# An FFT filter and a SiLU MLP in one kernel: a third staging buffer for the output weights, x behind the input weights, and part of the first MLP stretch moved one step later

## The chip, the cores and the metric

The kernel runs on one core of a Trainium2 chip. The metric is the device time of one execution in microseconds (us). The kernel before takes 776.0 us (median of 4 runs, 775.89 to 776.11). The profile counts a span from the first to the last instruction, which is 1.7 to 2.0 us shorter than the time. Ratios are computed as the mean time of one kernel's runs over that of the other's runs, so they are not quite the ratios of the medians that I quote.

PE is the matmul engine and PEld its weight load; DVE is VectorE, ACT is ScalarE, POOL is GpSimd, and SP is the engine that issues most DMAs.

## The reference

```python
X = np.fft.rfft(x, axis=1)                    # x: 8 x 3008 x 256
y = np.fft.irfft(X * (filt_r + 1j * filt_i)[None], n=3008, axis=1)
t = y.reshape(8 * 3008, 256)
h = t @ w_in                                  # 256 -> 2048
g = h * (1.0 / (1.0 + np.exp(-beta * h)))
out = g @ w_out                               # 2048 -> 256
```

## The kernel before

A prologue of about 33 us builds the transform tables and filters the first of eight batches. The MLP then runs as 752 steps; a step is one block of 128 hidden features for 512 tokens. In each step PE computes `hps` (two matmuls), ACT applies SiLU, and two steps later PE adds four `acc` matmuls with `w_out`. The transforms of the next batch are woven between them by a table of steps (`at(step, function, ...)`).

What the change touches: the output weights are loaded in four blocks of 512 KB into staging buffers (`ws`), and POOL divides each by beta into `wout_sb`; the input weights and x come by POOL's own DMA queue; the last units of the first batch's transform are finished inside the MLP ("late" turns: `z_late` is eight transposes on PE, called the z transposes here, and `f_late` the matmuls that read their result); `s1` is the first transform stage of the second batch and reads x (`xg`).

```python
wst = ctx.enter_context(tc.tile_pool(name="wstage", bufs=2, **tw))
...
for u in range(4):
    spread(u)                       # POOL copies of filter rows, each waits for filter loads
load_win(0, 4 * P)                  # input weights of steps 0 to 3, 256 KB
spread(4)
spread(5)
load_x(1, 0)
load_win(4 * P, FF)                 # input weights of steps 4 to 15, 768 KB
for g in range(1, 4):
    load_x(1, g)
load_wout(0)                        # SP's queue
load_wout(WG)
scale_wout(0)                       # POOL
scale_wout(WG)
...
at(0, z_late, 1, 0)
at(1, z_late, 1, 1)
s1_steps(1, range(16), [3 + (2 * i + 1) // 3 for i in range(16)], False, (1, 4, 7, 10, 13))
for i, r in enumerate((2, 3, 4, 5)):
    at(r, f_late, 1, i // 2, i % 2)
...
for f in (2, 3):
    at(f, load_wout, f * WG)
    at(f, scale_wout, f * WG)
```

`spin(n)` runs n matmuls on a tile that nobody reads; they fill PE's time just ahead of the MLP.

## Time and profile before

| | before |
|---|---|
| time, median | 776.0 us |
| span of the profiled run | 774.4 us |
| PE busy | 763.8 us (99%) |
| start of the first z transposes | 34.32 us |
| PE's empty issue time just before them | 0.44 us |
| PE's empty issue time at step 10, waiting for output weights | 0.89 us |

How to read it: PE is full nearly everywhere, so only PE's holes can be won. A hole is measured in issue time: the start of the next matmul, less the start of the last one and its usual distance to a successor (0.217 us for 512 columns, 0.109 for 256, 0.043 for 94 or 96). The profile's own "idle before" is shorter, because it counts from the modelled end of a matmul. The prediction shows the lines.

### The profile page before, as it was taken

The page shows a single profiled execution, that of the slowest core. Times are in us where ns is not written, and L with a number is a line of the kernel's source. Part 1 is how long each engine was busy: PE and PEld are TensorE (multiplying, and loading weights), DVE is VectorE, ACT ScalarE, POOL GpSimd, SP SyncE. Part 2 cuts the span into 40 slices and gives each one's busy share as a digit, 9 for nine tenths or more (in the row PEclk, how much of TensorE's full clock was granted, in tenths as well). Part 3 has the DMA queues.
Part 4 walks back from the last instruction along what each step waited for, and adds up shares of the span by engine and source line. Part 5 has one row for each costly group of instructions (what it writes and reads, how often), then busy time and mean ns, then how long its engine had stood idle before and what let it go on. Part 6 is the DMA issues. An engine that isn't in the chain of part 4 may idle for free.

```text
span 774.4 us, 15904 instructions
## 1 busy us (share of the span) xinstructions
PE 763.8 (99%) x6384; PEld 550.2 (71%) x6384; DVE 433.0 (56%) x716; ACT 552.2 (71%) x813; POOL 151.0 (20%) x154
## 2 busy tenths in 40 slices
PE   8899999999999999999999999999999999999997
PEld 5677777767777777867778777776777766676665
DVE  8868754766556655566556664566645665321001
ACT  7767877776677776777667777676676777777776
POOL 6714400312012210122201322022200222000000
PEclk9999999999999999999999999999999999999999
DMA  9968575234923248141671317621147111500101
GB/s 200 210 142 133 145 172 110 69 101 93 200 52 74 91 111 180 39 115 50 144 157 55 91 48 176 123 76 48 49 130 137 49 49 48 157 29 28 55 28 55
DMA packets 104125, 77.74 MB, mean 100 GB/s; under 512 B 49692, under 2 KB 97052, under 8 KB 104052
## 3 DMA queue, kind: packets, MB, share of 16 engines
q1 hardware_dynamic: 97652, 63.19, 31.3%
q0 software_dynamic: 4192, 13.40, 10.3%
q8 instruction: 50, 0.82, 0.4%
q10 hardware_dynamic: 2208, 0.14, 0.2%
q14 instruction: 23, 0.19, 0.1%
HBM read 43.46 MB, written 35.65 MB: 102 GB/s over the span
## 4 chain that ended last, share of the span: by engine, by line
PE 94%; DMA 2%; ACT 1%; DVE 1%; POOL 1%; issue 0%; DVEq 0%; POOLq 0%
PE acc L803 42%; PE hps L785 41%; PE ps L646 2%; PE ps L592 2%; PE ps L624 2%; PE ps L565 2%; DMA ws<-in_moe_w_out_dram 2%; POOL wout_sb L367 0%; PE sps L444 0%; ACT aT L110 0%; ACT t L110 0%; ACT y L110 0%; DVE u L226 0%; POOL xg L171 0%; PE sps L423 0%
## 5 line engine op out<-in xcount | busy, mean ns | idle before, releaser
L794 ACT ACTIVATE gT<-hps,beta_sb 128x512 bf16<-128x512 f32 x752 | 516.6, 687 | 209.4 <-PE hps L785 208.2
L803 PE MATMUL acc<-wout_sb,gT 128*128 128x256 bf16 x3008 | 453.2, 272 | 0.7 <-POOL wout_sb L367 0.7
L785 PE MATMUL hps<-y,win_sb 128*128 128x512 bf16 (+7 forms) x1728 | 447.8, 351 | 0.1
L803 PEld LDWEIGHTS <-gT 128*128 128x128 bf16 x3008 | 281.1, 98 | 102.9 <-issue 1.8
L611 POOL TENSOR_TENSOR yh<-a_t,b_t 128x512 bf16<-128x512 f32 x84 | 106.5, 1268 | 419.9 <-DVE b_t L610 419.5
L785 PEld LDWEIGHTS <-win_sb 128*128 128x128 bf16 x1728 | 164.8, 98 | 24.3 <-DVE y L114 0.3
L112 DVE COPY ost<-acc 128x512 f32<-128x512 f32 (+1 forms) x94 | 59.9, 679 | 139.8 <-PE acc L803 139.8
L114 DVE TENSOR_SCALAR y<-ps 128x376 bf16<-128x376 f32 (+2 forms) x128 | 63.3, 510 | 62.8 <-PE ps L646 59.1
L606 DVE TENSOR_TENSOR a_t<-ps,fr_sb 128x512 f32<-128x512 f32 x84 | 58.1, 692 | 67.8 <-PE ps L592 67.2
L112 DVE CAST a<-ps 128x384 bf16<-128x384 f32 x107 | 59.1, 556 | 58.0 <-PE ps L565 47.5
L607 DVE SCALAR_TENSOR_TENSOR b_t<-ps,fi_sb 64x512 f32<-64x512 f32 x84 | 58.2, 693 | 1.1
L610 DVE TENSOR_TENSOR b_t<-ps,fi_sb 64x512 f32<-64x512 f32 x84 | 57.4, 683 | 1.1
L112 DVE CAST z<-ps 128x512 bf16<-128x512 f32 x72 | 49.3, 685 | 1.9 <-PE ps L624 1.0
L646 PEld LDWEIGHTS <-zz 96*128 96x128 bf16 x448 | 29.7, 97 | 22.9
L565 PEld LDWEIGHTS <-xg 94*128 94x128 bf16 x448 | 30.4, 97 | 19.9
L565 PE MATMUL ps<-t,xg 94*128 94x96 bf16 x448 | 36.7, 205 | 0.0
L646 PE MATMUL ps<-t,zz 96*128 96x94 bf16 x448 | 34.7, 205 | 0.0
L592 PE MATMUL ps<-a,t 128*128 128x256 bf16 x168 | 32.1, 273 | 0.0
L624 PE MATMUL ps<-yh,t 128*128 128x256 bf16 x168 | 32.1, 273 | 0.0
L624 PEld LDWEIGHTS <-t 128*128 128x128 bf16 x168 | 16.2, 98 | 17.7 <-issue 0.6
L592 PEld LDWEIGHTS <-t 128*128 128x128 bf16 x168 | 16.1, 98 | 16.1
L171 POOL DMA_DIRECT2D xg<-in_x_dram x24 | 12.5, 524 | 54.9 <-PE ps L565 54.9
(95 smaller groups left out, 177.3 us busy)
## 6 DMA issues: line engine op xcount, KB each, us to landing
out_dram<-ost SPq DMA_DIRECT2D x42, 512.0 KB, 3.0
d<-z SPq DMA_DIRECT2D x28, 384.0 KB, 3.7
zz<-d SPq DMA_DIRECT2D x28, 384.0 KB, 6.8
xg<-in_x_dram POOLq DMA_DIRECT2D x24, 384.0 KB, 4.8
out_dram<-ost SPq DMA_DIRECT2D x9, 256.0 KB, 3.6
ws<-in_moe_w_out_dram SPq DMA_DIRECT2D x4, 512.0 KB, 9.2
fr_sb<-in_filt_r_dram SPq DMA_DIRECT2D x12, 128.0 KB, 4.4
fi_sb<-in_filt_i_dram SPq DMA_DIRECT2D x12, 128.0 KB, 4.3
```

Of the source, the lines that this page charges most:

```text
L112: nc.vector.tensor_copy(dst, src)
L114: nc.vector.tensor_scalar_mul(dst, src, scale)
L565: nc.tensor.matmul(ps[:, m * KP : (m + 1) * KP], lhsT=xg[b, g][:NP, m0 + m, e * P : (e + 1) * P], rhs=t1[:], start=True, stop=True,)
L592: nc.tensor.matmul(ps[:, e, :], lhsT=t2[:, k0 + e, :], rhs=st["a2", b, g][:, kk + e, :], start=True, stop=True,)
L606: nc.vector.tensor_tensor(a_t[:], ps[:], fr_sb[:, ks, :], ALU.mult)
L607: nc.vector.scalar_tensor_tensor(b_t[:M], ps[M:], -1.0, fi_sb[M:, ks, :], ALU.mult, ALU.mult)
L611: nc.gpsimd.tensor_tensor(yh[:], a_t[:], b_t[:], ALU.add)
L624: nc.tensor.matmul(ps[:, e, :], lhsT=t3[:, 2 * i + e, :P], rhs=yh[:, e, :], start=True, stop=True)
L646: nc.tensor.matmul(ps[:, e, :NP], lhsT=zz[:, j0 % JG + e, dc * P : (dc + 1) * P], rhs=t4[:], start=True, stop=True,)
L785: nc.tensor.matmul(hps[:, pos - t0 : pos - t0 + ln], lhsT=win_sb[:, dc, fb * P : (fb + 1) * P], rhs=ys[b][:, dc, n0 : n0 + ln], start=(dc ...
L794: nc.scalar.activation(gT[:], hps[:], ACT.Silu, scale=beta_sb[:, fb : fb + 1])
L803: nc.tensor.matmul(acc_of(i, tb)[:, tb % 2, :], lhsT=blk[i * NFB + fb][:, tb * P : (tb + 1) * P], rhs=wout_sb[:, fb, :], start=(fb == 0 an ...
```

## The change

The intent is to have the third block of output weights on the chip before PE needs it, to give PE a second pair of `hps` matmuls while VectorE still clears the banks of the prologue, and to make room for x, which now comes after the input weights.

```diff
-    wst = ctx.enter_context(tc.tile_pool(name="wstage", bufs=2, **tw))
+    wst = ctx.enter_context(tc.tile_pool(name="wstage", bufs=3, **tw))
...
-    load_x(1, 0)
     load_win(4 * P, FF)
-    for g in range(1, 4):
+    for g in range(4):
         load_x(1, g)
-    load_wout(0)
-    load_wout(WG)
+    for f0 in range(0, 3 * WG, WG):
+        load_wout(f0)
     scale_wout(0)
     scale_wout(WG)
...
-    spin(2, tail_tile(0, [P, 512]))
+    spin(1, tail_tile(0, [P, 512]))
...
-            at(0, z_late, 1, 0)
-            at(1, z_late, 1, 1)
-            s1_steps(1, range(16), [3 + (2 * i + 1) // 3 for i in range(16)], False, (1, 4, 7, 10, 13))
-            for i, r in enumerate((2, 3, 4, 5)):
+            at(1, z_late, 1, 0)
+            at(2, z_late, 1, 1)
+            s1_steps(1, range(16), [4 + (2 * i + 1) // 3 for i in range(16)], False, (1, 4, 7, 10, 13))
+            for i, r in enumerate((3, 4, 5, 6)):
...
-            for f in (2, 3):
-                at(f, load_wout, f * WG)
-                at(f, scale_wout, f * WG)
+            at(0, scale_wout, 2 * WG)
+            at(0, load_wout, 3 * WG)
+            at(1, scale_wout, 3 * WG)
```

I call the staging buffers part 1, the late turns and the spin part 2, and the new place of x with the later `s1` part 3.

## The prediction

> **What bounds the kernel now.** I read the page first: busy shares, then the chain that ended last.
>
> ```profile
> PE 763.8 (99%) x6384; PEld 550.2 (71%) x6384; DVE 433.0 (56%) x716; ACT 552.2 (71%) x813; POOL 151.0 (20%) x154
> ...
> PE 94%; DMA 2%; ACT 1%; DVE 1%; POOL 1%; issue 0%; DVEq 0%; POOLq 0%
> ```
>
> PE is busy for 99% of the 774.4 us span and is 94% of the chain. The only DMA on the chain is 2%, which the line shares give to the output weights (ws). No step of the MLP is added or removed, so the time can move only where PE stands still. I therefore looked for PE's holes next: the timeline of PE alone, around the start of the MLP (start us, us, engine, line, what, count, idle before).
>
> ```profile
> 32.80 0.60 PE L271 MATMUL pt<-rest 128*128 128x512 bf16 x2
> 33.45 0.59 PE L785 MATMUL hps<-y,win_sb 128*128 128x512 bf16 x2
> 34.32 0.61 PE L393 MATMUL tp<-ident,y 128*128 128x128 bf16 x8 [0.28 <-DVE y L114]
> 34.77 0.59 PE L785 MATMUL hps<-y,win_sb 128*128 128x512 bf16 x2
> 35.20 0.61 PE L393 MATMUL tp<-ident,y 128*128 128x128 bf16 x8
> 35.65 0.59 PE L785 MATMUL hps<-y,win_sb 128*128 128x512 bf16 x2
> 36.08 0.33 PE L398 MATMUL ps<-t,zz 96*128 96x94 bf16 x4
> 36.24 0.60 PE L803 MATMUL acc<-wout_sb,gT 128*128 128x256 bf16 x4
> ...
> 46.32 0.51 PE L565 MATMUL ps<-t,xg 94*128 94x96 bf16 x8
> 47.55 0.60 PE L803 MATMUL acc<-wout_sb,gT 128*128 128x256 bf16 x4 [0.73 <-POOL wout_sb L367]
> ```
>
> Two holes stand here. Differences of starts give what a packed group costs in PE's issue: an hps pair 0.43 (34.77 to 35.20), eight transposes 0.45 (34.32 to 34.77), four acc 0.44 (36.24 to 36.68), four of s1 or of a late turn 0.17 (36.08 to 36.24). The printed idle times count from the modelled end of the matmul before, so they are short. In issue slots the first hole is 34.32 - (33.45 + 0.43) = 0.44 us: the first z transposes wait for VectorE's last evictions from the banks that they reuse. The second is 47.55 - (46.32 + 2 x 0.17) = 0.89 us. From 48 us to the end I found no PE wait over 0.15 us; the waits view lists PE's acc waiting for wout_sb once and nothing else on PE in the MLP. The chain between 31 and 48 us tells what made the second hole:
>
> ```profile
> 31.18 1.90 POOL wout_sb L367
> 33.09 0.02 issue
> 33.10 12.44 DMA ws<-in_moe_w_out_dram
> 45.54 0.07 issue
> 45.61 1.90 POOL wout_sb L367
> 47.51 0.04 issue
> 47.55 0.60 PE acc L803 x4
> ```
>
> The third block of output weights is issued at 33.10, because only two staging buffers exist and the first is free when GpSimd has scaled it. It then takes 12.44 us, where the first took 5.2, and GpSimd needs 1.90 more.
>
> **What the Trainium skill says.** "DMA: Bandwidth & Descriptors", section "Queues, rings and completion order": each DMA engine serves the queue rows that have work in turn, and descriptors of one ring in ring order. The trace agrees in the main: the third block (SP's queue) waits while x and the input weights (GpSimd's queue) drain; its packets run in number only from 37 us and fast only from 43, when the other queue is empty. So a transfer's place in the order decides when it lands. "TensorE: Matmul & The Clock Gate", section "Back-to-back issue gap": about 216 ns between 512-column matmuls at full clock; half of my 0.43 per pair, so these stretches are packed and cannot be compressed. "SBUF — State Buffer", section "SBUF: two separate sides": VectorE and GpSimd lock each other out only where VectorE uses two SBUF ports. The moved scaling meets VectorE copies out of PSUM; the trace shows such a cast of 128x384 at 0.55 us with GpSimd busy (33.34) and 0.56 without (37.49), so I count no cost.
>
> **Part 1: three staging buffers, third load at once.** It is issued after the second, at about 23.5 instead of 33.1, and lies ahead of x. On SP's queue alone 512 KB take about 1.5 us (the queue moved some 0.17 to 0.18 MB per 0.5 us at 44 to 45 us). GpSimd scales three blocks back to back from 31.18: 31.18 + 3 x 1.89 = 36.9. PE needs the third at step 10, about 45. The 0.89 us hole goes. The fourth block is issued at 33.1, when the first buffer is free, so it inherits the old third's slow path: landed by 45.5, scaled by 47.5, needed at step 14, about 51. No new wait; gain 0.89.
>
> **Part 2: late turns a step later, one spin less.** The z transposes cannot start before 34.32, since VectorE's order ahead of them is unchanged. But the hps pair of step 1 now comes before them. With one spin, the first hps is freed about 0.22 earlier (at 33.24; it waits for the end of the last spin in the same bank); its second half waits for y until 33.48; step 1 then fills 33.70 to 34.13, and z starts at 34.32 as before. So 0.43 of useful work is moved into the hole: gain 0.43. The removed spin alone is worth nothing more, since VectorE sets 34.32; with two spins, 33.45 + 0.43 + 0.43 = 34.31 would fit too.
>
> **Part 3: x and the input weights swap places, s1 a step later.** From the landing times of narrow windows of the DMA view (KB each, median us to landing), the input weights issued at 28.8 and the first x at 28.3:
>
> ```profile
> win_sb<-in_moe_w_in_dram POOLq DMA_DIRECT2D x1, 768.0 KB, 8.5
> xg<-in_x_dram POOLq DMA_DIRECT2D x1, 384.0 KB, 4.6
> ```
>
> So before, x0 landed at 32.9 and the weights at 37.3, just in time for hps of step 4 at 37.89. Swapped, the weights land near 35 and x0 last of the pair, near 37.3. PE's order after the change, from 34.32: z 0.45, hps2 0.43, z 0.45, acc0 0.44, hps3 0.43, late turn 0.17, acc1 0.44, hps4 0.43, then s1 at 37.55, its weights loaded from 37.33. So x0 comes at its deadline. Two things move it: the inserted 512 KB push it back by up to 1.5 us, and the hole in the DMA traffic takes them up:
>
> ```profile
> 22.00:27.00 5.00, 4.77 (x61) 3.79 (x60) 5.00 (x5) 4.59 (x6) 4.78 (x6) 1.00 1.00 274
> 28.50:30.50 2.00, 1.77 (x29) 1.44 (x26) 1.56 (x3) 1.02 (x2) 2.00 (x4) 1.00 0.72 76
> ```
>
> The last column is GB/s: in 28.5 to 30.5 only 76 were moved against 274 just before, an idle worth of 2 x (1 - 76/274) = 1.44 us, about what ws needs. I estimate x0 at 37.3 to 37.8 and a new wait of 0.15 us (0 to 0.6). Later x keep their landings (about 39.7, 42.8, 45.2 by the same view) while their users come at steps 7, 9 and 12, about 41.8, 44 and 48, so they are free. The DMA transposes that follow s1 shift by less than a step and land about 5 us ahead of their reader at 61.86. The busier step 6 (s1, late turn and z turn in one) may cost 0.05 by waiting for a PSUM bank.
>
> Sum: -0.89 - 0.43 + 0.15 + 0.05 = -1.12, and PE has no later slack that could swallow it: 776.09 - 1.1 = 775.0.
>
> **Rivals.** (a) x0 is starved: if SP's queue with three weight blocks holds the software queue back (the first input weights, issued at 23.12, took 7.0 us for only 256 KB while SP's queue drained), x0 could land at 38 to 38.5 and PE waits 0.5 to 1.0 at step 4; time 775.4 to 775.9. For it: the deadline is that close. Against: the traffic hole, and the author's shift of s1. (b) The weight wait is only replaced: the fourth block comes too late. It would have to take over 15 us from 33.1; 11.9 and 12.4 were seen. If it did, 775.5 to 776. (c) The gain is lost later to a fixed-time transfer; against it, PE shows no such wait in the rest; would give 776. (d) x0 is early and VectorE frees the banks sooner: full gain, 774.7.
>
> **Range and chances.** The sum of holes caps the gain at 0.89 + 0.44 + 0.22 = 1.55, giving 774.5; (a) and (b) reach 775.9. Runs of one kernel spread by 0.2. Range 774.6 to 775.9. 2% is 15.5 us, ten times all holes together: same 0.98, and 0.01 for each side.
>
> **What would show it.** In the new profile: acc no longer waits for wout_sb, four scalings with the first three back to back ending near 36.9; ws third landing near 30; two hps pairs in a row before the first z transposes at 34.3; the first s1 near 37.6 with at most a short wait for x; the hps of step 4 without a wait for its weights. A wait of over 0.6 us at s1, or a new wait at the scaling of the fourth block, would make it wrong, as would a z start that leaves 34.3.

## The result, and the profile after

The changed kernel took 775.97 us in the median of 4 runs, against 776.0 us before. The ratio is 1.0 with a 95% interval of 0.9983 to 1.0017: the same, as the forecast of the class had it, but the median is 0.07 us outside the predicted range and the expected 1.0 us is missing. The single runs are 775.0, 777.1, 775.71 and 776.22; the four of before lie within 0.22 of each other. The profiled run is the first one, 775.0, which is the predicted time to the digit. So the trace in hand and the median tell different stories, and that is what had to be explained.

First the profiled run. Its page (busy time and instructions by engine; chain by engine):

```profile
PE 757.8 (98%) x6286; PEld 549.6 (71%) x6383; DVE 433.3 (56%) x716; ACT 552.3 (71%) x813; POOL 151.1 (20%) x154
...
PE 96%; ACT 1%; DVE 1%; issue 1%; POOL 0%; DVEq 0%; POOLq 0%
```

The DMA is off the chain. PE's busy time fell by 6 us only because 97 of the 6383 matmul records are missing from this trace (PEld has 6383, PE 6286; the third trace of this kernel has all 6383, and 763.9 us); a hole of exactly one missing matmul is no hole. Line numbers are one lower than before (L802 is the old L803). The timeline of PE in the same stretch, in the same columns as in the prediction:

```profile
32.81 0.38 PE L271 MATMUL pt<-rest 128*128 128x512 bf16 x1
33.24 1.07 PE L784 MATMUL hps<-y,win_sb 128*128 128x512 bf16 x3
34.33 0.61 PE L393 MATMUL tp<-ident,y 128*128 128x128 bf16 x8
...
37.13 0.59 PE L784 MATMUL hps<-y,win_sb 128*128 128x512 bf16 x2
37.56 0.34 PE L564 MATMUL ps<-t,xg 94*128 94x96 bf16 x4
...
46.76 0.51 PE L564 MATMUL ps<-t,xg 94*128 94x96 bf16 x8
47.10 0.60 PE L802 MATMUL acc<-wout_sb,gT 128*128 128x256 bf16 x4
```

The second `hps` pair now stands before z (four matmuls, one of them unrecorded), and z starts at 34.33, as predicted. The first `s1` runs at 37.56, straight after its `hps`. At step 10 `acc` follows `s1` without a gap (46.76 + 0.34 = 47.10). POOL's timeline shows the three scalings in one run, and the fourth far ahead of its use:

```profile
30.49 5.60 POOL L367 TENSOR_TENSOR wout_sb<-ws,rbeta_sb 128x1024 bf16<-128x1024 f32 x3
44.58 1.90 POOL L367 TENSOR_TENSOR wout_sb<-ws,rbeta_sb 128x1024 bf16<-128x1024 f32 x1 [8.48 <-DMA ws<-in_moe_w_out_dram]
```

The DMA hole of 28.5 to 30.5 us is filled, at 287 GB/s where it was 76 (135 in the third trace of the kernel before):

```profile
28.50:30.50 2.00, 1.77 (x30) 1.45 (x26) 1.57 (x3) 1.02 (x1) 1.94 (x5) 1.00 1.16 287
```

Comparing the starts of the SiLU instructions, step by step, the changed kernel is 1.32 us ahead from step 15 on and stays so to the end (1.33 at the last step). The sum of my two gains was 1.32. The difference of the spans is 774.38 - 773.05 = 1.33 us. In this run, then, nothing was lost at all. The question is why the other runs do not show it.

### The profile page after: what moved, and what is told of

Read it like the earlier page. It is cut to its first block, busy times and chain, and to the rows that moved or that the text cites. A ratio compares the mean times of both kernels' runs of the same rounds, so it can differ in the third digit from the quotient of the medians.

```text
span 773.0 us, 15801 instructions
## 1 busy us (share of the span) xinstructions
PE 757.8 (98%) x6286; PEld 549.6 (71%) x6383; DVE 433.3 (56%) x716; ACT 552.3 (71%) x813; POOL 151.1 (20%) x154
## 3 DMA queue, kind: packets, MB, share of 16 engines
q0 software_dynamic: 4192, 13.40, 10.2%
## 4 chain that ended last, share of the span: by engine, by line
PE 96%; ACT 1%; DVE 1%; issue 1%; POOL 0%; DVEq 0%; POOLq 0%
PE acc L802 44%; PE hps L784 39%; PE ps L645 3%; PE ps L564 3%; PE ps L591 3%; PE ps L623 3%; PE sps L444 0%; PE tp L393 0%; ACT aT L110 0%; ACT t L110 0%; ACT y L110 0%; PE ps L398 0%; DVE u L226 0%; DVE pq_t L430 0%; PE sps L423 0%
## 5 line engine op out<-in xcount | busy, mean ns | idle before, releaser
L802 PE MATMUL acc<-wout_sb,gT 128*128 128x256 bf16 x3008 | 453.2, 272 | 2.3
L784 PE MATMUL hps<-y,win_sb 128*128 128x512 bf16 (+7 forms) x1633 | 427.4, 350 | 0.1
L802 PEld LDWEIGHTS <-gT 128*128 128x128 bf16 x3008 | 281.0, 98 | 101.9 <-issue 0.9
```

The source lines that it names most:

```text
L784: nc.tensor.matmul(hps[:, pos - t0 : pos - t0 + ln], lhsT=win_sb[:, dc, fb * P : (fb + 1) * P], rhs=ys[b][:, dc, n0 : n0 + ln], start=(dc ...
L802: nc.tensor.matmul(acc_of(i, tb)[:, tb % 2, :], lhsT=blk[i * NFB + fb][:, tb * P : (tb + 1) * P], rhs=wout_sb[:, fb, :], start=(fb == 0 an ...
```

## The experiments

Three theories stood at the start. The other runs were scatter; or the change leans on DMA landings that differ from run to run, and the profiled run was a lucky one; or that session was noisy for any kernel. In the first two calls each timed experiment had five runs beside nine of the kernel before, on one chip per call; the third call is described in its place. The traces are of the first run of each.

### Both kernels again, unchanged

> The changed kernel once more, unchanged. Theory (the two holes are gone in every run, the other three runs were scatter): median 774.9 to 775.1, most runs within 0.3. Rival 1 (the change lives off DMA landings that differ from run to run; the profiled run was a lucky one): median 775.5 to 776.3, spread over 1 us, and where the profile falls in a slow run, PE waits 0.5 to 2 us for x (s1, step 4), for the input weights (hps, step 4) or for an output weight block. Rival 2 (that session was noisy for any kernel): spread under 0.4 here.

> The kernel before, unchanged, run as if it were a new one. Theory and rival 1: 775.9 to 776.1, spread under 0.4. Rival 2 (noise of the session): spread over 1 us here too.

Measured on one chip: changed kernel 775.97 (775.59 to 776.6), kernel before 776.39 over nine runs (775.74 to 777.09) and 775.98 as a new one (775.86 to 776.48, a spread of 0.62 where under 0.4 was expected). The ratio of the changed kernel is 0.9994 (0.9981 to 1.0006). So the kernel before scatters by over 1 us too (the third theory), but the changed kernel is again far from 774.9 (not the first). The traces differ from the earlier pair in just the disputed places. The changed kernel started z at 34.91 instead of 34.33, and waited 0.28 us for x. The kernel before waited much less for its third weight block than in the profile I had predicted from:

```profile
46.33 0.51 PE L565 MATMUL ps<-t,xg 94*128 94x96 bf16 x8
47.09 0.60 PE L803 MATMUL acc<-wout_sb,gT 128*128 128x256 bf16 x4 [0.26 <-POOL wout_sb L367]
```

In issue time that is 0.42 us instead of 0.89: the block landed at 45.07 instead of 45.54.

A second repetition, on another chip:

> The changed kernel a third time, for another trace. What is known: its first profile has z at 34.33 and no wait for x (span 773.05); its second has z at 34.91, a wait of 0.28 for x at step 4 and one of 0.2 at 134.8 (span 774.10). Theory A (the hole of before took up lateness of the prologue; without it lateness goes through to the end): span minus 773.05 equals the lateness of z against 34.33 plus the waits at s1 and at 134.8, within 0.1, whatever the run. Theory B (x lands at its deadline): the wait for x alone is over half of that difference.

> The kernel before, again, for another trace. Theory A: if z is late against 34.32, the wait for wout_sb at step 10 is shorter by that lateness (its end is set by the landing of the third block), so that the span changes less than the prologue. If z is on time, the wait is 0.4 to 0.9 by the landing at 45.0 to 45.6.

Measured: changed kernel 775.78 (775.63 to 776.22), before 775.93 over nine runs (775.53 to 776.66) and 775.87 as a new one. The ratio of the changed kernel is 0.9999 (0.9987 to 1.0012). The trace of the changed kernel has z on time, and this:

```profile
37.13 0.59 PE L784 MATMUL hps<-y,win_sb 128*128 128x512 bf16 x2
38.34 0.34 PE L564 MATMUL ps<-t,xg 94*128 94x96 bf16 x4 [0.62 <-DMA xg<-in_x_dram]
```

PE stands for 0.78 us of issue time (38.34 - 37.13 - 0.43) because x is not there. The wait in the kernel before was 0.52. The sum rule of theory A holds: 774.09 - 773.05 = 1.04, and the waits for x (0.78) and for yh later on (0.26) make 1.04.

### Part 1 alone, and parts 2 and 3 alone

```diff
# part 1 only: the kernel before, with
+ wstage bufs=3; load_wout(0), load_wout(WG), load_wout(2 * WG) at once
+ at(0, scale_wout, 2 * WG); at(0, load_wout, 3 * WG); at(1, scale_wout, 3 * WG)
# parts 2 and 3 only: the changed kernel, with these lines as in the kernel before
```

> On the kernel before, only part 1: three staging buffers, the third block loaded at once; late turns, spins, x order and s1 as before. Theory: the 0.89 us hole at step 10 is gone, the 0.44 us hole stays; the input weights land at about 37.5 and hps of step 4 waits 0 to 0.4; 775.1 to 775.6. Rival 1 (unstable landings come with the third block ahead of x): spread over 1 us here as well, median near 776.

> The changed kernel with part 1 undone: two staging buffers, the third block loaded late; late turns, spin, x order and s1 as changed. Theory: the 0.43 us won before z is lost again at step 10, where acc now waits about 1.3 us for the third block, whose landing at about 45.5 does not move; 775.9 to 776.1, no gain alone. If the gains added up instead it would be 775.6. Rival 1 (instability from x moved behind the weights): spread over 1 us here.

Measured beside the 776.39 above: part 1 alone 776.09 (775.46 to 777.11), parts 2 and 3 alone 776.62 (776.11 to 776.95). Both lie above what was expected (775.1 to 775.6, and 775.9 to 776.1); part 1 alone has the spread of over 1 us that rival 1 named. The trace of part 1 alone has no wait for output weights, z at 34.33 with its hole before it, and a span of 773.51, or 0.87 below the first profile of before: that term is real in the trace. But this trace is of the fastest of the five runs, and POOL was early in it (its last filter copy starts at 26.67, against 27.29 in the first profile of before). Even so the input weights landed only at 37.87, just ahead of their reader at 37.91: they took 9.68 us from their issue, against 8.32 to 9.03 in the four traces of before. So what stands behind the third block does come later here. Parts 2 and 3 alone lose both ways:

```profile
38.75 0.34 PE L564 MATMUL ps<-t,xg 94*128 94x96 bf16 x4 [0.98 <-DMA xg<-in_x_dram]
...
47.72 0.60 PE L802 MATMUL acc<-wout_sb,gT 128*128 128x256 bf16 x4 [0.46 <-POOL wout_sb L367]
```

x comes 1.14 us late in issue time although no third weight block lies ahead of it here. So in this one trace the extra 512 KB were not needed to make x late; standing behind the 768 KB of input weights was enough. `acc` then waits 0.63 us of issue time and not the expected 1.3, because the wait for x comes first.

### x first again; and the input weights cut in two

```diff
# x first: the changed kernel with
-    load_win(4 * P, FF)
-    for g in range(4):
+    load_x(1, 0)
+    load_win(4 * P, FF)
+    for g in range(1, 4):
# cut in two: the changed kernel with
-    load_win(4 * P, FF)
-    for g in range(4):
+    load_win(4 * P, 8 * P)
+    load_x(1, 0)
+    load_win(8 * P, FF)
+    for g in range(1, 4):
         load_x(1, g)
```

> The changed kernel with the first x ahead of the input weights again, as in the kernel before. hps of step 4 now needs its weights at 37.1 and they land at 37.3 to 38: PE waits 0.3 to 0.9 there, no wait for x at s1. So 0.2 to 0.6 slower than the changed kernel if order mattered; if x and weights land at random, the same.

> The changed kernel with the second load of input weights cut in two: 256 KB for steps 4 to 7, then the first x, then 512 KB for steps 8 to 15. Theory B: x lands near 35, input weights near 32.5 and 37.5, no wait at step 4 in any run; mean 0.2 to 0.5 faster than the changed kernel, mean span near 773.7. Theory A: the waits for x are a small part; prologue lateness stays; gain 0 to 0.2.

Measured in the same call as the second repetition (changed kernel 775.78, before 775.93). With x first: 776.61 (776.25 to 777.15), 0.83 above the changed kernel where 0.2 to 0.6 was expected. The wait only changes its name, and is larger (1.56 us of issue time):

```profile
36.68 0.60 PE L803 MATMUL acc<-wout_sb,gT 128*128 128x256 bf16 x4
38.68 0.60 PE L785 MATMUL hps<-y,win_sb 128*128 128x512 bf16 x2 [1.40 <-DMA win_sb<-in_moe_w_in_dram]
```

The order of x and input weights is that of the kernel before, with the third block ahead of them, and the weights took 9.9 us from their issue, where the prediction shows 8.5:

```profile
win_sb<-in_moe_w_in_dram POOLq DMA_DIRECT2D x1, 768.0 KB, 9.9
```

With part 1 alone this makes two traces, one each of two versions, in which what follows the third block lands late.

Cut in two: 775.25 (775.10 to 775.44), the first version with all runs of its call below the changed kernel's. x landed at 35.10, the first piece of weights at 33.22, and step 4 waits for nothing:

```profile
37.13 0.59 PE L786 MATMUL hps<-y,win_sb 128*128 128x512 bf16 x2
37.56 0.34 PE L566 MATMUL ps<-t,xg 94*128 94x96 bf16 x4
```

This fits theory B, at more than its predicted size (0.2 to 0.5 in the mean; the means differ by 0.66, the medians by 0.53). The spread is 0.34 here, but 0.99 in the repeat below. The wait for x is a large part of what the changed kernel loses; the table of traces below says how large.

### What each part is worth once x is out of the way

Four versions of the cut-in-two kernel: unchanged; with two staging buffers; with part 2 undone; with the second spin put back.

```diff
# two buffers: bufs=2, third and fourth block loaded and scaled as in the kernel before
# old turns: spin(2), z_late at steps 0 and 1, f_late from 2, s1 from 3
# second spin:
-    spin(1, tail_tile(0, [P, 512]))
+    spin(2, tail_tile(0, [P, 512]))
```

> The version with the input weights cut in two, again, on another chip. Theory (x no longer at its deadline): 775.0 to 775.5 against 775.8 to 776.3 of the kernel before, all runs within 0.5. If the first result was luck: 775.6 to 776.2.

> The same with part 1 undone (two staging buffers, third block late). Theory: the wait for the third block ends where its landing puts it, so it eats what the late turns won; wait at step 10 of 0.85 to 1.3 instead of 0.4 to 0.9; time that of the kernel before within 0.2, so 0.5 to 0.9 above the split version. Rival (the gains are separate): only 0.4 to 0.6 above it, with a wait of 0.4 to 0.6.

> The same with part 2 undone (late turns, s1 and the second spin as in the kernel before; three buffers kept). Theory: the 0.44 hole before the first z transposes is back, nothing else; 0.4 to 0.5 above the split version. Rival (the hole is refilled by slack later): the same as the split version within 0.1.

> The same with the second spin matmul put back alone. Theory: VectorE sets the start of the first z transposes at 34.32 to 34.33, both hps pairs still fit before it (33.45, 33.88, end at 34.31); z does not move, time as the split version within 0.15. Rival (the removed spin was worth its 0.22): 0.2 above.

This call fell on the same chip as the one before, not on another, and nine of the ten runs of the kernel before (median 775.92) are those of the earlier call; one is new (775.89). The versions had four to six runs:

| version | median | lowest to highest |
|---|---|---|
| cut in two, again | 775.31 | 774.99 to 775.98 |
| two buffers | 777.04 | 776.37 to 779.19 |
| old turns | 775.95 | 775.51 to 776.40 |
| second spin | 775.20 | 775.10 to 775.69 |

The repeat agrees with the first in the median (ratio 0.9993, interval 0.9979 to 1.0006; the interval still holds 1), though not in the spread: its runs do not lie within 0.5. With two buffers (four runs; the one of 779.19 has a granted clock of 0.997) the wait at step 10 is larger than I expected:

```profile
45.90 0.34 PE L566 MATMUL ps<-t,xg 94*128 94x96 bf16 x4
48.08 0.60 PE L804 MATMUL acc<-wout_sb,gT 128*128 128x256 bf16 x4 [1.85 <-POOL wout_sb L367]
```

That is 2.01 us of issue time. The theory that the landing sets the end is right, since 48.08 is near the 47.55 of before, but the end moved by 0.5: POOL issues one DMA more in this version and was late by 0.3 in this run, so it frees the first buffer at 34.14 instead of 33.10, and the third block lands at 46.06 instead of 45.54. So in this trace part 1 would have been worth about 2 us. The ratio of this version to the kernel before, 1.0019 (1.0005 to 1.0032), is the only one of all here whose interval leaves out 1. Both of my figures for this run were too low.

With the old turns the hole before z is back at its size:

```profile
33.88 0.59 PE L786 MATMUL hps<-y,win_sb 128*128 128x512 bf16 x2
34.75 0.61 PE L393 MATMUL tp<-ident,y 128*128 128x128 bf16 x8 [0.28 <-DVE y L114]
```

34.75 - 33.88 - 0.43 = 0.44 us. The medians differ by 0.64 from the repeat and 0.70 from the first, where 0.4 to 0.5 was expected; the prologue of the traced run was late by 0.43 as well, which is not part of the edit. The second spin leaves z at 34.32, and costs 0.10 us in its trace, because the first SiLU is later and the third `hps` pair starts at 34.87 instead of 34.77; in the times it can't be seen.

### Three more traces of the changed kernel and one of before

By then it was open how the loss splits in a typical run, and how large the removed wait is in a typical run.

> The changed kernel, one more trace. If the wait for x is its main loss: x lands at 37.9 to 38.7 and s1 waits 0.3 to 1.1 in most of these three traces. If the first trace (no wait) is typical: x before 37.5 in two of three. Span minus 773.05 equals lateness of z plus the waits for x and for yh.

> The changed kernel, the second of three more traces; the same expectation as for the first: x at 37.9 to 38.7 and a wait of 0.3 to 1.1 if x is the main loss, x before 37.5 and none if the first trace was typical.

> The changed kernel, the third of three more traces; the same expectation: x at 37.9 to 38.7 and a wait of 0.3 to 1.1 if x is the main loss, x before 37.5 and none if the first trace was typical.

> The kernel before, one more trace. If the 0.89 of the first profile was at the long end: the wait for wout_sb is 0.4 to 0.6, as in the two later profiles. If 0.89 was typical: 0.8 to 1.0.

Times (one run each, state unknown): 776.15, 775.99, 775.68; before 775.85, and 776.54 for the run of the kernel before that the call made beside them. All ten traces of the two kernels, in us (x issued and landed: the first x; z late: against 34.33; waits in issue time; `yh` is what POOL adds up of the filtered values, and PE's next transform reads it):

| trace | x issued | x landed | z late | wait for x | wait for wout_sb | wait for yh | span |
|---|---|---|---|---|---|---|---|
| changed, first profile | 28.36 | 37.42 | 0 | 0 | none | 0 | 773.05 |
| changed, again | 29.71 | 38.37 | 0.58 | 0.28 | none | 0.20 | 774.10 |
| changed, third | 29.09 | 38.29 | 0 | 0.78 | none | 0.26 | 774.09 |
| changed, fourth | 29.26 | 38.64 | 0.14 | 0.99 | none | 0 | 774.20 |
| changed, fifth | 29.57 | 38.04 | 0.44 | 0.09 | none | 0.37 | 773.96 |
| changed, sixth | 29.33 | 38.18 | 0.20 | 0.47 | none | 0 | 773.74 |
| before, first profile | 28.27 | 32.90 | 0 | none | 0.89 | 0 | 774.38 |
| before, again | 28.26 | 32.82 | 0 | none | 0.42 | 0.21 | 774.10 |
| before, third | 28.13 | 33.15 | 0 | none | 0.52 | 0 | 774.01 |
| before, fourth | 28.49 | 32.86 | 0.08 | none | 0.51 | 0 | 774.07 |

The rows of the changed kernel add up: span minus 773.05 equals the three losses within 0.02 us in every row. x landed after 37.9 in five traces of six; in four of them the expected range of the wait (0.3 to 1.1) or nearly so was met, in the fifth a late z left only 0.09. The 0.89 of the first profile of before was the long end; the three others lie at 0.42 to 0.52.

So of the 0.81 us that the six traces lost in the mean, the wait for x is 0.44, a late z 0.23 and yh 0.14; the wait for x is over half of the loss in three of the five traces that lost something.

The table also tells why the first profile was lucky. x lands 8.5 to 9.4 us after its issue, and POOL issued it at 28.36 in that run and at 29.09 to 29.71 in the others. POOL issues x after its filter copies, and those wait for filter loads. The waits of POOL between 12 and 30 us (us in total, times, longest), first in the first profile, then in the second trace:

```profile
POOL fi_sb L473 <- DMA fi_sb<-in_filt_i_dram: 0.4, 1, 0.4
```

```profile
POOL fi_sb L473 <- DMA fi_sb<-in_filt_i_dram: 1.8, 1, 1.8
```

The longer wait ended at 18.47, well before the first output weights are issued (22 to 23 us), so the change did not make it. It delays x, and z as well. In all ten traces z is late by what the start of POOL's last filter copy exceeds 27.43 us, within 0.02: copies at 27.39, 27.56, 27.63, 27.86 and 28.01 in the changed kernel go with 0, 0.14, 0.20, 0.44 and 0.58 (in the fourth trace of before 27.51 goes with 0.08). In the first profile that copy started at 26.66, 0.77 earlier than this, while z came no earlier than 34.33. So x gained on its reader in that run alone.

Among the other five a late issue is no wait by itself, because the reader of x moves along with z. There the wait follows the time from issue to landing: 8.47, 8.66, 8.85, 9.20 and 9.38 us go with waits of 0.09, 0.28, 0.47, 0.78 and 0.99. The pair of x and the input weights took 9.2 to 10.1 us from the first issue to the last landing in the six traces (mean 9.66), against 8.9 to 9.6 in the four of before (mean 9.09). It took 10.2 with part 1 alone, 10.4 with x first, and 10.2 with parts 2 and 3 alone, in one trace each. So the third block and the new order each went with a longer time; why is not shown.

The wait for yh stands at about 134 us in both kernels. It follows how long the eight DMA transposes of the third batch take: from first issue to last landing 13.8 us in the first profile of the changed kernel (no wait), 14.1 in its third trace (0.26), 14.2 in the cut-in-two kernel (0.33), 14.1 in the second trace of before (0.21). The last one of these lines of PE, from the cut-in-two kernel:

```profile
133.49 0.60 PE L786 MATMUL hps<-y,win_sb 128*128 128x448 bf16 x4
134.26 0.38 PE L625 MATMUL ps<-yh,t 128*128 128x256 bf16 x2 [0.17 <-POOL yh L612]
```

I ran nothing on why the transposes vary.

## Why the prediction was right or wrong

- **The hole before z (0.43).** Right. z starts at 34.33 where POOL's filter copies are not late, both `hps` pairs stand before it in all traces, and the hole of 0.44 comes back when part 2 is undone.
- **The spin.** Nearly right: alone it is worth 0.10 us in a trace, not 0, and invisible in the times.
- **The weight wait (0.89).** The mechanism was right and the size was off. The wait is gone in every trace with three buffers, but 0.89 was read from a single trace; the mean of four is 0.59. This term was too large by 0.30.
- **"x0 comes at its deadline", "a new wait of 0.15 us (0 to 0.6)".** This is the step that failed. The prediction let x land near where the pair of x and input weights had ended in one trace, at 37.3 to 37.8, because the DMA hole would take up the 512 KB put ahead. The hole was filled (76 to 287 GB/s), but x landed at 38.04 to 38.64 in five traces of six (mean of the six 38.16), and PE waited 0.44 us for it in the mean, up to 0.99. In the four traces of before the pair ended at 37.38 in the mean. Of the 0.78 us between, 0.57 is the longer time of the pair and 0.21 POOL's later start. Rival (a) named this outcome. Its cause, the third block, is neither shown nor excluded: two traces with the old order show the weights behind that block late, and parts 2 and 3 alone show x late without it.
- **"PE has no later slack that could swallow it".** Not quite. The wait for yh costs 0 to 0.37 in the changed kernel and 0.21 once in four traces before, a small piece of what rival (c) named. The bank wait of 0.05 at step 6 was in no trace.
- **A term I did not have: a late prologue.** "A z start that leaves 34.3" was a sign of being wrong, and z left it in four traces of six. It costs 0.23 us in the mean of the changed kernel's traces, 0.02 in those of before. Its cause lies before the change acts, so I take the difference for chance; four and six traces do not prove it.

With the measured terms the sum reads -0.59 - 0.43 + 0.44 + 0.21 (late z, the difference of the means) + 0.09 (yh, likewise, 0.14 - 0.05) = -0.28. That is 0.84 less gain than the predicted 1.12: 0.30 from the weight wait, 0.29 from x, 0.21 from z and 0.09 from yh, less the 0.05 of step 6 that did not come. The mean span of the six traces is 773.86 and that of the four of before 774.14, a difference of -0.28. In the timed calls the means differ by about 0, -0.4 (-0.1 against the kernel before as a new one) and 0. So a gain of some 0.3 us is possible and not shown. The profiled 775.0 met the prediction by luck: the one trace of the changed kernel with POOL early stood against the one trace of before with the longest weight wait.

- **The range (774.6 to 775.9).** It took a scatter of 0.2 us, which is that of the four runs of the kernel before (0.22). Nine runs of that kernel in a later call spread over 1.35 us.

The experiments did point to a better version: with the input weights cut in two the median was 775.25 and 775.31 on one chip, against 775.93 of the kernel before (mostly the same runs both times) and 775.78 of the changed one: 0.5 to 0.7 us below. It is under a thousandth of the time, and the intervals still touch 1.

## What to carry to other kernels

A wait that one trace shows has a size for that run only; before a gain is booked, read the same wait in a second and third trace. When a load is moved to a place in the order where it lands exactly at its reader, its jitter becomes time: an early landing gains nothing there and a late one costs, as x did in five of six traces. If the reader moves with the issue, look at the time from issue to landing, not at the issue. Cutting the larger transfer ahead of it, so that each piece comes before its own first reader, removed the wait for x in the traces taken.

## What the Trainium skill lacked or had wrong

- "DMA: Bandwidth & Descriptors", section "Queues, rings and completion order", has each DMA engine take turns between queue rows, a packet at a time. In the kernel before that fits from 37 us on: SP's queue, with the third output weight block, moved 129 packets to 136 of POOL's in 37 to 40 us, and 152 to 145 in 40 to 43 (about 1 KB each against 3.6 KB, so POOL moved most of the bytes). But the block was issued at 33.10, and from then to 37.0 SP's queue moved no packet, against 240 of POOL's. How long a newly issued transfer stands behind what another queue already holds is not on the page; the block took 12.4 us to land here, against 5.2 for the first.
- No page tells how far the landing of the same load varies between runs of one kernel: the first x took 8.5 to 9.4 us from its issue in six runs, and its issue varied by 1.35 us.
- "TensorE: Matmul & The Clock Gate", section "Back-to-back issue gap", gives about 131 ns per matmul of 512 columns and 81 of 128 for a stream of matmuls that each load their weights, and calls the 216 and 56 ns of its formula the gaps of an isolated matmul. Here every matmul has a weight load (6384 of each), the granted clock is 1.00, and the stream shows 217 ns (an `hps` pair in 0.43) and 56 ns (eight transposes in 0.45), so the formula is met and the figures for a stream are not.
- "Perfetto Trace Analysis" does not warn of missing matmul records: 97 of 6383 are absent from the profile after. 95 of them are `hps` matmuls, and each looks like a hole of 0.21 us.
